# Holding the split of the first group's x in fixed order at the end of its step, in a recurrence with a feed-forward block

## The chip, the cores and the metric

One core of a Trainium2 chip. The metric is the device time of one execution, in microseconds (us).

The engines in the profile: PE is TensorE (its matmuls; PEld are its weight loads), DVE is VectorE, ACT is ScalarE, POOL is GpSimd, and SP is the sync engine, whose queue issues most loads. L405 is line 405 of the kernel before. The granted clock (PEclk) is the share of its full clock that PE was given; "half clock" is a share of 0.5.

## The reference

```python
# q, k, v, alpha: (4, 8, 768, 48) float32; w1, w2: (384, 1024); w3: (1024, 1024); w_out: (1024, 384), float64
state = zeros((B, H, D, D))
for t in range(S):                                   # S = 768
    state = alpha[:, :, t, :, None] * state + einsum('bhd,bhe->bhde', k[:, :, t], v[:, :, t])
    y[:, :, t] = einsum('bhd,bhde->bhe', q[:, :, t], state)
x = y.transpose(0, 2, 1, 3).reshape(3072, 384)
out = (((x @ w1) * (x @ w2)) @ w3) @ w_out           # (3072, 384)
```

## The kernel before

The recurrence runs in 24 steps, one per chunk of 128 rows of one batch. Step n works on several chunks at once: scores of chunk n, transposes of chunk n+1, logarithms and decays of chunks n+3 and n+4. Four chunks make a group g of x, which goes out to DRAM in `attend` and comes back transposed with `load_x`. `split_x` splits it into three parts for exact matmuls: one operation on ACT (L405) and two on DVE (L406, L407). A *gate piece* is nine matmuls (six L416, three L420) on these parts. Gate pieces are pushed between the steps of the recurrence by `run`. The weights come as 64-bit words and are converted in `to_fp32`, a few instructions at a time (`convert`).

The order of instructions in the source is a priority, not the final order. A scheduler places each instruction when its own plan says that its inputs are ready. `keep_order(True, instruction)` holds an instruction at its place in the source. Each engine then works through its own list in order (the prediction shows it on ACT).

```python
def to_fp32(dst, *srcs):
    # ... raw tile, loads on the sync queue
    first = st.setdefault("raw", 0) < 3              # only three conversions are held in order
    st["raw"] += 1
    keep_order(first, nc.scalar.activation(rest, low, AF.Copy, scale=2.0 ** -52))        # L201
    # ... L202, L206 on DVE, L208 on ACT, then L210 to L213 on DVE; ends in L221 (ACT), L223, L224 (DVE)

def attend(n):
    # ...
    for half in range(2):
        if g:
            later.append((to[half, :, :, ds(c * C, C)], x[ds(DP * half, D)]))            # sync queue, next step
        else:
            nc.gpsimd.dma_start(out=to[half, :, :, ds(c * C, C)], in_=x[ds(DP * half, D)])  # POOL's queue

def load_x(g, queue=nc.sync):
    st["xT", g] = xp.tile([C, KM, TG], FP32, tag="xT", name="xT")
    queue.dma_start(out=st["xT", g], in_=xd[g].rearrange("(k p) t -> p k t", p=C))       # L399

def split_x(g, i):
    x = st.pop(("xT", g))
    t = tr[i].tile([C, 3, KM, TG], FP32R, tag="x3", name="x3")
    st["x3", g] = t
    nc.scalar.activation(t[:, 0], x, AF.Copy, scale=1.0 - 2.0 ** -13)                    # L405
    nc.vector.tensor_sub(t[:, 1], x, t[:, 0].bitcast(FP32))                              # L406
    nc.vector.scalar_tensor_tensor(t[:, 2], t[:, 0].bitcast(FP32), 1.0 + 1.0 / P, x,     # L407
                                   op0=ALU.mult, op1=ALU.subtract)

for n in range(N + 1):
    # ... store(), loads of later chunks
    if n:
        attend_state(n - 1)                          # L375
    if n < N:
        scores(n)                                    # L356 on PE, L359 on DVE
    transposed(n + 1)                                # L316 on PE, L318 on ACT
    if n - 2 in begin:                               # group 0: n = 6
        g, tiles = begin[n - 2]
        split_x(g, 0)
        fill.extend(gate(g, f) for f in tiles)
    pieces = ((0, 0, 1), (1, 1, 1), (1, 1, 0), (1, 1, 0))[(n - 6) % 4] if n > 5 else (0, 0, 0)
    # ... logs
    decayed(n + 2)                                   # L294 on DVE, from q and k
    convert(1, 2 if n == 0 else 3)
    advance(n)
    if n in begin:
        load_x(begin[n][0], nc.gpsimd)               # group 0: n = 4
    if n:
        attend(n - 1)                                # L381 on PE, L385 on ACT
    outer(n)                                         # L328 on PE
    run(pieces[0])
    convert(n > 0)
    run(pieces[1])
    decays(n + 3)                                    # L278 on PE, L284 and L285 on ACT
    convert(n < 9)
    run(pieces[2])
```

## Time and profile before

| what | before |
|---|---|
| time, median of 3 runs | 495.98 us (494.5 to 497.73) |
| PE busy in the profiled execution | 469.7 us of 496.0 us |
| the one long wait: ACT at L405 for x of group 0 | 8.1 us, ending at 54.05 us |
| from the scores (L356) of step 5 to those of step 6 | 11.7 us |
| from step 6 to step 7, and from 7 to 8 | 8.2 us and 8.9 us |

Every step has one group of sixteen L356 matmuls, so their starts are a clock for the recurrence. A step that takes 11.7 us where its neighbours take 6 to 9 has a hole. The profile's lines are in the prediction below. A list of waits has, for each engine and line, what released it, then the total wait, how often, and the longest. A timeline has the start in us from the span's start, the duration, engine, line, operation, output and input, and in brackets the idle time just before and what ended it.

### The profile page before, as it was taken

The page shows a single profiled execution, that of the slowest core. Times are in us where ns is not written, and L with a number is a line of the kernel's source. Part 1 is how long each engine was busy: PE and PEld are TensorE (multiplying, and loading weights), DVE is VectorE, ACT ScalarE, POOL GpSimd, SP SyncE. Part 2 cuts the span into 40 slices and gives each one's busy share as a digit, 9 for nine tenths or more (in the row PEclk, how much of TensorE's full clock was granted, in tenths as well). Part 3 has the DMA queues.
Part 4 walks back from the last instruction along what each step waited for, and adds up shares of the span by engine and source line. Part 5 has one row for each costly group of instructions (what it writes and reads, how often), then busy time and mean ns, then how long its engine had stood idle before and what let it go on. Part 6 is the DMA issues. An engine that isn't in the chain of part 4 may idle for free.

```text
span 496.0 us, 9941 instructions
## 1 busy us (share of the span) xinstructions
PE 469.7 (95%) x3774; PEld 427.1 (86%) x3774; DVE 372.1 (75%) x621; ACT 248.2 (50%) x479; POOL 45.8 (9%) x94
## 2 busy tenths in 40 slices
PE   7787599999899989999999999999999999999996
PEld 3566499798899879999999988888888999999996
DVE  3579599999988646999999769686434786677771
ACT  4565577678667443555565445454223533333330
POOL 3244032211302210000000000000000000000000
PEclk9788699999899989999999999999999999999999
DMA  9999999989998823456646433320001885555511
GB/s 169 203 209 223 216 204 260 197 205 222 217 211 183 230 82 112 117 196 197 196 156 196 155 116 113 121 93 32 33 32 51 227 231 176 176 176 175 174 49 48
DMA packets 158255, 79.10 MB, mean 159 GB/s; under 512 B 104640, under 2 KB 151232, under 8 KB 158208
## 3 DMA queue, kind: packets, MB, share of 16 engines
q1 hardware_dynamic: 155920, 74.86, 59.6%
q0 software_dynamic: 2288, 3.62, 2.9%
q8 instruction: 29, 0.48, 0.4%
q14 instruction: 18, 0.15, 0.1%
HBM read 56.40 MB, written 22.06 MB: 158 GB/s over the span
## 4 chain that ended last, share of the span: by engine, by line
PE 69%; DVE 3%; DMA 2%; issue 1%; SPq 1%; ACT 1%; DVEq 0%; ACTq 0%
PE bank L416 36%; PE bank L420 18%; PE bank L465 8%; PE bank L381 2%; DMA raw<-in_moe_w_out_dram 2%; PE bank L459 1%; PE bank L356 1%; PE bank L375 1%; DVE ms L359 1%; PE bank L316 1%; SPq L439 1%; DVE x L407 1%; PE bank L328 0%; DVE x L406 0%; DVE qk L294 0%
## 5 line engine op out<-in xcount | busy, mean ns | idle before, releaser
L416 PE MATMUL bank<-x,w 128*128 128x384 f32 x768 | 160.2, 343 | 1.2 <-DVE ms L359 1.2
L416 PEld LDWEIGHTS bank<-x,w 128*128 128x128 f32 x768 | 134.3, 189 | 6.0 <-DVE ms L359 2.0
L418 ACT ACTIVATE t<-bank 128x384 f32<-128x384 f32 x152 | 74.4, 491 | 113.6 <-PE bank L416 104.3
L421 DVE SCALAR_TENSOR_TENSOR r<-bank,t 128x384 f32<-128x384 f32 x128 | 69.4, 552 | 38.0 <-ACT t L418 27.6
L420 PE MATMUL bank<-x,w 128*128 128x384 f32 x384 | 87.8, 336 | 1.7 <-DVE x L407 1.3
L420 PEld LDWEIGHTS bank<-x,w 128*128 128x128 f32 x384 | 68.2, 188 | 3.1 <-DVE x L407 1.6
L416 PE MATMUL bank<-w3o,ab 128*128 128x384 f32 x384 | 70.4, 334 | 0.0
L416 PEld LDWEIGHTS bank<-w3o,ab 128*128 128x128 f32 x384 | 66.9, 188 | 0.0
L465 PE MATMUL bank<-wo,w3T 128*128 128x384 f32 x128 | 42.6, 486 | 0.0
L201 ACT ACTIVATE rest<-raw 128x512 f32<-128x512 uint32 (+1 forms) x36 | 23.4, 651 | 28.1 <-DMA raw<-in_moe_w_dram 19.7
L356 PE MATMUL bank<-qkT 48*128 48x128 f32 x384 | 31.1, 304 | 6.7 <-ACT qkT L318 6.3
L420 PE MATMUL bank<-w3o,ab 128*128 128x384 f32 x192 | 37.1, 334 | 0.0
L465 PEld LDWEIGHTS bank<-wo,w3T 128*128 128x128 f32 x128 | 24.2, 189 | 14.9
L356 PEld LDWEIGHTS bank<-qkT 48*128 48x128 f32 x384 | 25.8, 203 | 12.6 <-ACT qkT L318 7.2
L484 DVE TENSOR_TENSOR ab<-abl,ab 128x1024 fp32r<-128x1024 f32 x24 | 29.3, 1223 | 9.1 <-ACT ab L483 9.1
L432 DVE TENSOR_TENSOR ab<-r 128x384 f32<-128x384 f32 x64 | 35.4, 553 | 0.9
L483 ACT ACTIVATE ab<-abl 128x1024 fp32r<-128x1024 f32 x24 | 25.5, 1062 | 18.8 <-PE bank L420 18.8
L420 PEld LDWEIGHTS bank<-w3o,ab 128*128 128x128 f32 x192 | 33.6, 188 | 0.0
L208 ACT ACTIVATE power<-power,rebias 128x512 uint32<-128x512 uint32 (+1 forms) x36 | 25.0, 697 | 15.8 <-DVE power L206 15.5
L359 DVE TENSOR_TENSOR ms<-bank,keep 128x512 int32<-128x512 int32 x48 | 30.8, 680 | 1.1 <-PE bank L356 1.1
L294 DVE TENSOR_TENSOR qk<-kq,e 128x768 f32<-128x768 f32 x24 | 22.8, 951 | 11.4 <-ACT e L285 6.4
L318 ACT COPY qkT<-bank 128x512 f32<-128x512 f32 x48 | 25.7, 587 | 10.2 <-PE bank L316 10.2
(74 smaller groups left out, 548.5 us busy)
## 6 DMA issues: line engine op xcount, KB each, us to landing
abd<-ab SPq DMA_DIRECT2D x64, 192.0 KB, 2.5
abl<-abd SPq DMA_DIRECT2D x24, 512.0 KB, 4.5
raw<-in_moe_w_dram SPq DMA_DIRECT2D x16, 512.0 KB, 4.2
raw<-in_moe_w_dram SPq DMA_DIRECT2D x24, 256.0 KB, 4.9
ac<-in_alpha_dram SPq DMA_DIRECT2D x24, 192.0 KB, 4.5
kq<-in_k_dram SPq DMA_DIRECT2D x24, 192.0 KB, 5.0
kq<-in_q_dram SPq DMA_DIRECT2D x24, 192.0 KB, 5.0
v<-in_v_dram SPq DMA_DIRECT2D x24, 192.0 KB, 4.5
```

The lines of the kernel that those rows point to most:

```text
L208: keep_order(first, nc.scalar.activation(power, power, AF.Relu, scale=2.0 ** 23, bias=rebias))
L318: keep_order(n < 2, nc.scalar.copy(qkT[:, :, :, ds(DP * half, DP)], tp[half]))
L356: nc.tensor.matmul(sc[i][:, j, :], qkT[r, 0, j, :], qkT[r, 1, j, :], start=True, stop=True)
L359: nc.vector.tensor_tensor(ms[:, i].bitcast(I32), sc[i].bitcast(I32), keep_bc, op=ALU.bitwise_and)
L416: nc.tensor.matmul(p1, w[part][i], x[part][i], start=(part == i == 0), stop=(part == 1 and i == n - 1))
L418: nc.scalar.activation(t, p1, AF.Copy, scale=(1.0 + 1.0 / P) * scale)
L420: nc.tensor.matmul(p2, w[2][i], x[2][i], start=(i == 0), stop=(i == n - 1))
L421: nc.vector.scalar_tensor_tensor(to, p2, -scale, t, op0=ALU.mult, op1=ALU.add)
L432: nc.vector.tensor_mul(ab, *r)
L465: nc.tensor.matmul(po, w3T[:, j, :], wo[:, j, :], start=(j == 0), stop=(j == KF - 1))
L483: nc.scalar.activation(t[:, 0], ab, AF.Copy, scale=1.0 - 2.0 ** -13)
L484: nc.vector.tensor_sub(t[:, 1], ab, t[:, 0].bitcast(FP32))
```

## The change

The intent is to take the split of group 0 off the place where ACT waits for x. It is moved from the middle of step 6 to its end, and held there so that the scheduler can't place it early. The other splits stay as they were.

```diff
-    def split_x(g, i):
+    def split_x(g, i, fixed=False):
...
-        nc.scalar.activation(t[:, 0], x, AF.Copy, scale=1.0 - 2.0 ** -13)
-        nc.vector.tensor_sub(t[:, 1], x, t[:, 0].bitcast(FP32))
+        keep_order(fixed, nc.scalar.activation(t[:, 0], x, AF.Copy, scale=1.0 - 2.0 ** -13))
+        keep_order(fixed, nc.vector.tensor_sub(t[:, 1], x, t[:, 0].bitcast(FP32)))
...
-    begin = {4 + 4 * g: (g, range(FH if g < 4 else KF)) for g in range(5)}
+    first = 4
+    begin = {first + 4 * g: (g, range(FH if g < 4 else KF)) for g in range(5)}
+
+    def visit(n, fixed=False):
+        g, tiles = begin[n]
+        split_x(g, 0, fixed)
+        fill.extend(gate(g, f) for f in tiles)
...
-        if n - 2 in begin:
-            g, tiles = begin[n - 2]
-            split_x(g, 0)
-            fill.extend(gate(g, f) for f in tiles)
+        if n - 2 in begin and n - 2 > first:
+            visit(n - 2)
...
         convert(n < 9)
+        if n - 2 == first:
+            visit(first, True)
         run(pieces[2])
```

## The prediction

> **What bounds the kernel now.** I read the page first (busy shares, slices, groups), then the list of waits, then the timeline of each engine around the first split of x, and last the busy time by stretch. The kernel has two parts: an attention recurrence of 24 steps (up to about 200 us) with pieces of the feed-forward block pushed between its steps, then the rest of the feed-forward block and the output projection.
>
> The page says that PE is the bound of the whole:
>
> ```profile
> PE 469.7 (95%) x3774; PEld 427.1 (86%) x3774; DVE 372.1 (75%) x621; ACT 248.2 (50%) x479; POOL 45.8 (9%) x94
> PE   7787599999899989999999999999999999999996
> DVE  3579599999988646999999769686434786677771
> PEclk9788699999899989999999999999999999999999
> DMA  9999999989998823456646433320001885555511
> ```
>
> The span less PE's busy time is 26 us of idle PE. One slice is 12.4 us. From slice 5 on PE is nearly full, so what is lost before that isn't made up. The fifth slice (49.6 to 62 us) is the odd one: PE and DVE at half, and a low granted clock. The list of waits for 51 to 58 us says why, as waiting engine, line, releaser, and us in total, times, longest:
>
> ```profile
> ACT x L405 <- DMA xT<-xd: 8.1, 1, 8.1
> DVE w L223 <- ACT w L221: 6.2, 1, 6.2
> PE bank L356 <- ACT qkT L318: 6.0, 1, 6.0
> ```
>
> L405 is the first instruction of the split of x for group 0 (the group's x has gone out to DRAM and is read back transposed). All twelve splits run L405, and this is the only one whose wait shows. The timeline of ACT shows what stood behind it, and the timelines of POOL and PE what it hung on and what hung on it:
>
> ```profile
> 45.41 0.50 ACT L285 ACTIVATE e<-bank 128x384 f32<-128x384 f32 x1
> 54.05 1.16 ACT L405 ACTIVATE x<-xT 128x1152 fp32r<-128x1152 f32 x1 [8.13 <-DMA xT<-xd]
> 55.11 0.61 ACT L221 ACTIVATE w<-mant 128x512 fp32r<-128x512 f32 x1
> 56.18 1.06 ACT L318 COPY qkT<-bank 128x512 f32<-128x512 f32 x2
> ...
> 47.55 0.80 POOL L399 DMA_DIRECT2D xT<-xd  x1 [2.63 <-DMA xd<-x]
> ...
> 57.29 2.08 PE L356 MATMUL bank<-qkT 48*128 48x128 f32 x16 [6.04 <-ACT qkT L318]
> ```
>
> The split belongs to step 6 of the source, but in the emitted order it stands ahead of the L318 copies of step 5 (the transposed q and k of chunk 6, without which the scores of step 6 can't start). So the instruction order is not the source order: whatever places the instructions thought x would be there by 46 us. The load was only issued at 47.55 and landed at 54.0. PE and DVE ran out of work 4 to 5 us after ACT stopped, and all three stood until 54 to 57 us.
>
> Next, what limits the stretches around it (us from:to, length, busy us and count of PE, PEld, DVE, ACT, POOL, then PE clock, DMA share, GB/s):
>
> ```profile
> 38.00:51.30 13.30, 10.29 (x150) 8.15 (x148) 10.75 (x18) 7.04 (x15) 5.56 (x8) 0.87 1.08 233
> 51.30:57.30 6.00, 0.01 (x2) 0.01 (x2) 1.54 (x3) 3.25 (x6) 0.00 (x0) 0.64 0.85 187
> 57.30:64.00 6.70, 6.70 (x68) 6.23 (x69) 6.70 (x11) 4.52 (x12) 1.62 (x3) 0.56 1.05 237
> 64.00:80.00 16.00, 16.00 (x196) 14.83 (x195) 15.84 (x31) 12.45 (x28) 5.16 (x10) 1.00 1.06 208
> 80.00:100.00 20.00, 18.80 (x268) 16.74 (x267) 19.73 (x35) 13.56 (x29) 3.31 (x7) 1.00 1.00 228
> ```
>
> From 57 to 100 us DVE is busy 42.3 of 42.7 us and PE 41.5: both engines have no room. So a microsecond given back to both before that is a microsecond at the end, as far as the loads keep up. DMA is near its limit all along.
>
> **What the Trainium skill says.** (1) "PSUM — Partial Sum Buffer", section "Engine vs sequencer instructions": the queues of ScalarE, VectorE and GpSimd are strict FIFO. The trace agrees: no ACT instruction starts between 45.41 and 54.05, though the L318 copies that follow had had their transposes finished at about 48.0 (PE's L316 ends there). (2) "TensorE: Matmul & The Clock Gate", section "What's actually happening": the array runs at half clock after an idle window of about 3.4 us and at full clock after a busy one. The trace agrees: the clock is 0.56 in 57.3 to 64, and the sixteen L356 matmuls take 2.08 us there against 1.16 at 74 us. (3) "DMA: Bandwidth & Descriptors", section "Specifications": transfers need 512 B or more for full rate. In 44 to 75 us 18,898 of 21,151 packets are under 512 B, and the engines' share is full at a mean of 219 GB/s.
>
> **The change, part by part.** It adds no instruction and takes none away. It moves the split of group 0 alone from the middle of step 6 to its end, and holds its ACT operation (1.16 us) and its first DVE operation (1.35 us) in source order, so they can't be placed early. The other eleven splits stay where they are.
>
> (a) The wait goes. ACT can go on at 45.9 with L221, L201 and the L318 copies; the scores of step 6 can follow at once on PE's L375, which ends at 51.25. DVE gets back up to 6.15 us, PE up to 6.04. Gain up to **6.1 us**. By the end of step 6 (about 58 us on the new timetable: 51.3 plus a step of 6 to 7 us, the spacing of the L356 groups before the wait) the load has been there for 4 us, so the moved split should not wait.
>
> (b) Loads. Before the wait the steps are paced by loads: in the trace's landing records, chunks 6 to 8 of alpha land 0.1, 0.5 and 0.1 us before ACT's L263 reads them. While the engines stood, the sync queue went on issuing (its waits on engines in 44 to 57 us sum to 0.9 us), so after the wait alpha is 5.4, 5.7, 5.3, 5.5 and 4.2 us early for chunks 10 to 14, and the raw weights of the sixth and seventh conversion 3.3 and 4.0 us. That lead was bought by the wait. If all engines move 6 us forward and the transfers don't, the smallest of these fall short by 2 to 3 us. Some comes back, as the sync queue waits on engines for 4 us in 57 to 75 us and for 6 us in 75 to 104, and these waits shorten. ACT and DVE can also go ahead with little queued work. I take **1.6 us** back (a choice between 0 and 3).
>
> (c) The split at the end. The first gate piece needs L405, L406 and, for its last three matmuls, L407: 1.16 + 1.35 + 1.35 = 3.9 us after the last exponential of step 6. Before, these ran in the shadow of the wait and DVE's part pushed the L359 masks to 60.18. If PE takes the gate piece ahead of the scores of step 7 it stands for up to 3 us; if those scores are placed first it loses nothing, and the placement does like to fill holes. I take **0.6 us**.
>
> (d) Clock. With the hole gone the half-clock stretch of 53 to 63 us shortens. PE's step-6 groups took some 2.4 us longer than at full clock, but DVE was full in that stretch, so most was hidden. Gain **0.3 us**.
>
> Sum: 6.1 - 1.6 - 0.6 + 0.3 = 4.2 us, so 495.98 - 4.2 = **491.8 us**.
>
> **Rivals.** R1, the loads take over: alpha, q/k and the raw weights become the pace again in steps 6 to 10. For it: DMA at its limit and the leads of near zero before the wait. Against it: no engine but POOL waits on a DMA from 57 to 160 us, and the leads of 5 us. Gain then 1 to 3 us, 493 to 495. R2, the end of the step becomes the new wait: PE stands for the split chain and DVE for L405. For it: the order is fixed and PE takes its matmuls in order. Against it: independent scores and transposes of step 7 can be put into the hole. Gain then 2 to 3.5 us. R3, everything carries through, clock too: 6 us and up to 2 more, 488 to 490. For it: PE and DVE are full afterwards and the rest of the kernel is PE work of fixed amount. R4, the placement of all later instructions shifts, as it works forward from this point, with a microsecond or two either way; the profile can't tell.
>
> **Range and chances.** The three runs of before lie between 494.5 and 497.7, so the reference itself moves by 1.5 us. R1 and R2 together give the upper end, R3 the lower: **488.5 to 495.5**. Faster by over 2% needs 486.1, that is 9.9 us, more than the whole wait with its clock effect: 0.04. Slower by over 2% needs 10 us of new waits: 0.02. Within 2%: 0.94.
>
> **What would show it.** In the changed profile: the ACT wait on xT at L405 is under 1 us and the split starts at 56 to 60 us; PE's L356 of step 6 starts at 51 to 52 us instead of 57.3; the fifth slice of PE and DVE rises to 8 or 9. For (b): alpha's L263 and the L201 conversions of steps 6 to 9 show DMA waits of 0 to 3 us in all. For (c): a PE wait ahead of the first L416 or L420, on ACT's L405 or on DVE's L406 or L407. For the carrying through: the last attention step ends some 4 us earlier and the part after 200 us keeps its length. I'm wrong if those waits on loads or on the split take over 4 us, if x lands later than now because its load or its stores move in POOL's queue, or if other instructions are placed worse.

## The result

| | before | with the change |
|---|---|---|
| median, 4 runs each | 496.23 us (494.5 to 497.73) | 501.55 us (500.27 to 501.8) |
| ratio of the fast runs | | 1.0103, 95% interval 1.0066 to 1.0141 |
| profiled execution (that of before is a further one) | 497.82 us | 500.27 us |

A ratio here is the mean time of one kernel's fast runs over that of the other's of the same rounds, so it isn't quite the ratio of the medians quoted. The change is slower by 1.0%, inside "within 2%", but on the other side of zero from the prediction of 491.8 us and outside its range. A repeat with more rounds (label after_again) gave 502.48 us against 495.99, ratio 1.0132 (1.0085 to 1.018), as expected; its profile was the 912 us execution and isn't used. The text on record for it:

> The change once more, as a reference for the other three of this batch on the same chip. Both theories: 1.005 to 1.015 of the kernel before, as in the first comparison.

The page of the changed kernel has the same work (busy times of the engines, and rows of tenths by slice):

```profile
PE 470.5 (94%) x3774; PEld 425.2 (85%) x3774; DVE 371.6 (75%) x621; ACT 247.6 (50%) x479; POOL 45.3 (9%) x94
PE   8888389899899999999999999999999999999996
DVE  3578789996967866899999869776434687777771
PEclk9788869999999999999999999999999999999999
```

The hole is still in the fifth slice, and deeper: PE's digit there is a 3, where it was a 5 before and where the prediction asked for 8 or 9. DVE's went from 5 to 7. PE's busy time as a whole is as before (470.5 and 469.7 us), so what the change costs is mostly idle PE (28.0 us against 26.3 in the two traces). A slice of 12.5 us hides what happened inside it, and the windows cut it finer. These are the same stretches as in the prediction (from:to, length, busy us and count of PE, PEld, DVE, ACT, POOL, then PE clock, DMA share, GB/s), of the changed kernel:

```profile
51.30:57.30 6.00, 3.97 (x66) 3.23 (x66) 3.10 (x6) 3.73 (x9) 1.13 (x2) 1.00 0.90 220
57.30:64.00 6.70, 0.80 (x2) 0.80 (x3) 6.67 (x13) 5.50 (x11) 2.44 (x6) 0.58 1.20 222
64.00:80.00 16.00, 15.32 (x147) 13.31 (x148) 13.97 (x24) 8.59 (x18) 2.21 (x4) 0.75 0.93 213
```

PE gained 4.0 us of work in the first stretch and lost 5.9 in the second (0.80 against 6.70 before). The changed kernel's waits for 51 to 70 us say why:

```profile
PE bank L416 <- ACT x L405: 7.5, 1, 7.5
ACT rest L201 <- DMA raw<-in_moe_w_dram: 4.9, 2, 3.1
DVE qk L294 <- ACT qkT L318: 2.9, 1, 2.9
```

ACT's wait on x is gone from this list, and PE has one of 7.5 us on the split instead. PE's timeline shows where it stands. First the kernel before:

```profile
62.88 1.08 PE L278 MATMUL bank<-la,utri 128*128 128x384 f32 x2
63.50 1.52 PE L416 MATMUL bank<-x,w 128*128 128x384 f32 x6
64.86 0.68 PE L420 MATMUL bank<-x,w 128*128 128x384 f32 x3
65.48 1.16 PE L356 MATMUL bank<-qkT 48*128 48x128 f32 x16
```

and the changed kernel:

```profile
51.78 1.16 PE L356 MATMUL bank<-qkT 48*128 48x128 f32 x16 [1.39 <-ACT qkT L318]
...
54.84 0.91 PE L278 MATMUL bank<-la,utri 128*128 128x384 f32 x2
63.20 1.33 PE L416 MATMUL bank<-x,w 128*128 128x384 f32 x3 [7.45 <-ACT x L405]
65.18 1.33 PE L416 MATMUL bank<-x,w 128*128 128x384 f32 x3 [0.65 <-DVE x L406]
66.53 1.30 PE L420 MATMUL bank<-x,w 128*128 128x384 f32 x3
67.76 2.08 PE L356 MATMUL bank<-qkT 48*128 48x128 f32 x16
```

The order on PE is the same in both: decays (L278), first gate piece (L416, L420), then the scores of step 7 (L356). In the kernel before, the split had been done in time and the gate piece ran at once. In the changed one PE reaches the gate piece at 55.75 us and stands there till 63.2, with the scores of step 7 behind it.

ACT's timeline of the changed kernel shows why the split is so late:

```profile
53.91 1.11 ACT L318 COPY qkT<-bank 128x512 f32<-128x512 f32 x2
58.17 0.68 ACT L201 ACTIVATE rest<-raw 128x512 f32<-128x512 uint32 x1 [3.14 <-DMA raw<-in_moe_w_dram]
58.75 0.62 ACT L221 ACTIVATE w<-mant 128x512 fp32r<-128x512 f32 x1
...
61.56 0.52 ACT L267 CAST la<-la 128x384 fp32r<-128x384 f32 x1
61.96 1.18 ACT L405 ACTIVATE x<-xT 128x1152 fp32r<-128x1152 f32 x1
```

L405 carries no wait: x was there. But ahead of it in ACT's order stands L201, the first ACT operation of the sixth weight conversion. The source has it in step 7, the scheduler had placed it ahead of the held split, and its raw weights landed only at 58.09 (it starts at 58.17). ACT stood 3.14 us for them and then worked 3.8 us (58.17 to 61.96) on other things before the split came.

DVE's two operations of the split end at 60.3 us in the kernel before (57.64 and 58.91, 1.35 us each), and at 66.4 in the changed one:

```profile
55.08 0.96 DVE L294 TENSOR_TENSOR qk<-kq,e 128x768 f32<-128x768 f32 x1 [2.90 <-ACT qkT L318]
...
63.77 1.35 DVE L406 TENSOR_TENSOR x<-xT,x 128x1152 fp32r<-128x1152 f32 x1
65.04 1.35 DVE L407 SCALAR_TENSOR_TENSOR x<-x,xT 128x1152 fp32r<-128x1152 f32 x1
```

The wait ahead of L294 is put down to ACT's L318, which ended at 55.02. But a semaphore instruction of DVE just before L294 waits for q and k of chunk 8, and in the trace's landing records q of chunk 8 lands at 54.95; DVE gets past this instruction at 55.03. So up to 54.95 the wait is one on a load, and only the last 0.1 us can be ACT's.

The starts of the scores, in us after the first matmul (1.2 us less than in the timelines), give the whole account:

| scores of step | 5 | 6 | 7 | 8 | 9 | 14 | 20 | 23 | last instruction |
|---|---|---|---|---|---|---|---|---|---|
| before | 44.4 | 56.1 | 64.3 | 73.2 | 80.7 | 118.9 | 165.3 | 190.2 | 494.8 |
| change | 43.5 | 50.6 | 66.6 | 77.4 | 84.8 | 123.3 | 172.3 | 192.7 | 497.2 |
| difference | -0.8 | -5.5 | +2.3 | +4.2 | +4.1 | +4.3 | +7.0 | +2.4 | +2.4 |

By step 6 the change is 5.5 us ahead: 4.7 us are won from step 5 to 6 (7.0 us instead of 11.7), and 0.8 us it was ahead at step 5 already, before anything differs. Then 7.8 us are lost from step 6 to 7 (16.0 us instead of 8.2), and another 1.9 from 7 to 8 (10.8 instead of 8.9). From there the difference is carried on, moving between 2.4 and 7.0 us. The two profiled executions differ by less (2.4 us) than the medians (5.3), since the profiled execution of before was a slow one among its runs and that of the change its fastest.

### The profile page after: what moved, and what is told of

Read it like the earlier page. It is cut to its first block, busy times and chain, and to the rows that moved or that the text cites.

```text
span 498.5 us, 9954 instructions
## 1 busy us (share of the span) xinstructions
PE 470.5 (94%) x3774; PEld 425.2 (85%) x3774; DVE 371.6 (75%) x621; ACT 247.6 (50%) x479; POOL 45.3 (9%) x94
## 4 chain that ended last, share of the span: by engine, by line
PE 74%; DVE 9%; DMA 8%; issue 4%; ACT 3%; SPq 1%; POOL 1%; ACTq 0%; DVEq 0%; POOLq 0%
PE bank L416 37%; PE bank L420 18%; PE bank L465 8%; DMA raw<-in_moe_w_out_dram 3%; PE bank L356 2%; DMA raw<-in_moe_w_dram 2%; PE bank L381 2%; DVE qk L294 2%; DVE ms L359 2%; PE bank L459 1%; PE bank L316 1%; DMA kq<-in_k_dram 1%; PE bank L146 1%; PE bank L375 1%; DMA dec<-ends 1%
## 5 line engine op out<-in xcount | busy, mean ns | idle before, releaser
L416 PE MATMUL bank<-x,w 128*128 128x384 f32 x768 | 160.5, 343 | 11.2 <-ACT x L405 7.5
L416 PEld LDWEIGHTS bank<-x,w 128*128 128x128 f32 x768 | 134.5, 189 | 16.7 <-ACT x L405 8.1
L420 PE MATMUL bank<-x,w 128*128 128x384 f32 x384 | 88.3, 337 | 2.3 <-DVE x L407 1.3
L420 PEld LDWEIGHTS bank<-x,w 128*128 128x128 f32 x384 | 68.4, 189 | 4.3 <-PE bank L416 2.4
L416 PE MATMUL bank<-w3o,ab 128*128 128x384 f32 x384 | 70.4, 334 | 0.0
L416 PEld LDWEIGHTS bank<-w3o,ab 128*128 128x128 f32 x384 | 66.9, 188 | 0.0
L201 ACT ACTIVATE rest<-raw 128x512 f32<-128x512 uint32 (+1 forms) x36 | 23.4, 651 | 34.0 <-DMA raw<-in_moe_w_dram 25.7
L420 PE MATMUL bank<-w3o,ab 128*128 128x384 f32 x192 | 37.1, 334 | 0.0
L356 PE MATMUL bank<-qkT 48*128 48x128 f32 x384 | 32.3, 309 | 2.2 <-ACT qkT L318 1.7
L356 PEld LDWEIGHTS bank<-qkT 48*128 48x128 f32 x384 | 26.9, 208 | 8.5 <-issue 4.0
L420 PEld LDWEIGHTS bank<-w3o,ab 128*128 128x128 f32 x192 | 33.6, 188 | 0.0
L294 DVE TENSOR_TENSOR qk<-kq,e 128x768 f32<-128x768 f32 x24 | 22.9, 953 | 14.3 <-ACT e L285 8.3
L318 ACT COPY qkT<-bank 128x512 f32<-128x512 f32 x48 | 25.7, 591 | 9.2 <-PE bank L316 9.0
```

Of the source, the lines that this page charges most:

```text
L294: nc.vector.tensor_mul(qks[n % 3][:, :, :, 0:D], st.pop(("kq", n)), st.pop(("e", n)).rearrange("p i (h d) -> p i h d", h=H))
L318: keep_order(n < 2, nc.scalar.copy(qkT[:, :, :, ds(DP * half, DP)], tp[half]))
L356: nc.tensor.matmul(sc[i][:, j, :], qkT[r, 0, j, :], qkT[r, 1, j, :], start=True, stop=True)
L416: nc.tensor.matmul(p1, w[part][i], x[part][i], start=(part == i == 0), stop=(part == 1 and i == n - 1))
L420: nc.tensor.matmul(p2, w[2][i], x[2][i], start=(i == 0), stop=(i == n - 1))
```

## The experiments

**Theories.** *Order*: holding the split makes everything in ACT's queue ahead of it part of its path, and PE takes the gate piece ahead of the scores; the loss is this chain. *Loads* (rival): work moved forward, transfers didn't, so the wait comes back at loads of q, k and raw weights. *Clock* (rival): PE's idle time sits just ahead of a dense stretch, and the half clock after it is what costs. *Placement* (rival): something elsewhere was placed worse. The texts number theories: T1 is order, T2 loads alone, T3 PE's order alone, T4 clock, and T5 that the end of the split sets the time. Rounds are three for the first six and five for the rest, and "before" is the kernel before in the same rounds on the same chip. Edits are against the change where not said otherwise. Step starts are from one traced execution each. In the traces of kernels whose order is the same up to step 5, the scores of that step start at 42.9 to 45.2 us, so a difference of one or two microseconds between two traces isn't safe.

### 1. Which half of the change acts: place or hold

**end_free**: the split at the end of the step, but not held.

```diff
-            visit(first, True)
+            visit(first, False)
```

> The split moved to the end of the step but not held in order. In the built order its ACT operation stands where it stood before the change, so both theories expect the wait of about 8 us on the load of x and the time of the kernel before, 495 to 498 us: the hold in order, not the place in the source, is what acts.

Measured: 496.58 us (496.09 to 497.73), ratio 0.9994 (0.9936 to 1.0051). Compared with the kernel before, the order is the same on all engines but DVE, where the split's two operations and their neighbours have changed places (L407 ends at 63.65 us instead of 60.26). The old waits are there (46 to 80 us):

```profile
ACT x L405 <- DMA xT<-xd: 7.6, 1, 7.6
...
PE bank L356 <- ACT qkT L318: 7.2, 1, 7.2
```

So the move in the source does nothing to the time by itself. The result comes from the hold.

**mid_fixed**: the split held at its old place in the middle of step 6.

```diff
-        if n - 2 in begin and n - 2 > first:
-            visit(n - 2)
+        if n - 2 in begin:
+            visit(n - 2, n - 2 == first)
...
-        if n - 2 == first:
-            visit(first, True)
```

> The change with the split left at its old place in the middle of step 6, but held in order there. In the built order the split's ACT operation then stands right behind the copies of the transposed q and k of chunk 7 and ahead of the conversion that waits for raw weights. Theory T1 (the change loses because the split stands in ACT's queue behind a conversion that waits for its load and behind the rest of step 6, while PE takes its first gate matmuls in order ahead of the scores of step 7): the split starts at 54 to 57 us, PE's wait ahead of the first L416 falls from 7.5 us to 1 to 4 us, the scores of step 7 start at 60 to 65 us after the first matmul instead of 66.6, total 490 to 496 us, below the change by 6 us or more. Rival T2 (the loads alone set the pace of steps 6 to 8 and no order can beat it): the scores of step 7 start at 66 us or later and the total stays at 499 to 502.

Measured: 497.85 us (497.46 to 498.96), ratio 1.0013 (0.9946 to 1.0081). The split starts at 54.1 us after the first matmul (change: 60.8), and the gate piece stands for less:

```profile
PE bank L416 <- DVE x L406: 2.6, 1, 2.6
```

Scores of step 7 at 62.2 and of step 8 at 72.4, earlier than before by 2.1 and 0.8 us. The steps behaved as expected, the total (490 to 496) didn't: it is level with before. Against the change this is 3.7 us better by the medians, which are of different rounds (by the ratios, 1.0013 and 1.0103, about 0.9%). So a longer queue ahead of the held split is part of the loss.

### 2. The consumer: is the gate piece ahead of the scores the loss?

**gate_late**: the change, with the first gate piece moved from the end of step 6 into step 7.

```diff
-        pieces = (...)[(n - 6) % 4] if n > 5 else (0, 0, 0)
+        pieces = (...)[(n - 6) % 4] if n > 7 else (2, 1, 1) if n == 7 else (0, 0, 0)
```

> The change, with the first gate piece run in step 7 (two pieces there after its outer products) and not at the end of step 6, so that PE takes the scores, transposes and attention of step 7 before it. T1: PE's 7.5 us wait ahead of the first L416 shrinks to 2 to 5 us, the scores of step 7 start at 55 to 58 us after the first matmul, and the total is 494 to 498 us, 3 to 7 us under the change. T2 (loads alone): the time lost moves to waits of ACT and DVE on loads in step 7, and the total stays within 2 us of the change's 501.5.

Measured: 497.02 us (496.5 to 497.93), ratio 1.0001 (0.9944 to 1.0058). The scores of step 7 start at 57.4 instead of 66.6, and the wait ahead of the gate piece shrinks:

```profile
DVE qk L294 <- DMA kq<-in_q_dram: 3.5, 1, 3.5
...
PE bank L416 <- ACT x L405: 1.6, 1, 1.6
```

The ranges that the theory of order gave for the total and for step 7 hold, and the wait is shorter than the 2 to 5 us expected. But the scores of step 8 start at 74.2, 1.0 us later than before: the split is no earlier (63.27 us, in the change 61.96), and all of the gate work of the two steps now stands ahead of the scores of step 8.

**before_gate_late**: the control, the same edit on the kernel before.

> Control: the kernel before, with the first gate piece after the outer products of step 7 and nothing else. There the split is done by the time PE gets to the gate piece, so moving it should neither win nor lose: 495 to 499 us, ratio 0.995 to 1.006. If it wins 1% by itself, the gain seen with the gate piece moved is not the undoing of the change's loss but a gain of its own.

Measured: 495.0 us (494.09 to 499.94), ratio 0.9993 (0.9944 to 1.0041). The edit by itself is worth nothing, so what it gives back on top of the change is a loss of the change.

**mid_gate_late** and **mid_gate_late5** (a repeat with five rounds): the edits of mid_fixed and gate_late together.

> Both edits: the split held in order in the middle of step 6, and the first gate piece after the outer products of step 7. T1: no PE wait over 2 us at 55 to 65 us, the 5.5 us won at the scores of step 6 are kept to the end apart from load waits, total 488 to 493 us. T2: 496 us or more.

> The version with the split held in the middle of step 6 and the first gate piece in step 7, once more with five rounds: its four runs lay between 493 and 500 us, though its traced run was 4.6 us ahead of the traced run of before. Theory T5 (what counts is when the split is done and with it the gate pieces, not when ACT's wait on x is gone: in the traces the split's last operation ends 59.1 us after the first matmul before, 65.2 in the change, 64.9 with both places undone at the end of the step, 61.1 here): 0.988 to 0.997 of before. Otherwise 0.997 to 1.006.

Measured: 498.15 us (493.21 to 500.04), ratio 1.0007 (0.9926 to 1.0087), and 496.48 (493.96 to 499.77), ratio 0.9992 (0.995 to 1.0034). Both traces show scores of step 8 some 4.5 us earlier than before (68.3 and 68.8), but the traced executions took 493.21 and 494.82 us, the fastest of four and the third of six, and others of the same kernel took up to 500. An expectation of 488 to 493 was missed, and the repeat (by T5 0.988 to 0.997) doesn't support a gain. A warning: a trace of one execution told a better story than the mean of the runs.

### 3. The queue ahead: the conversion that was placed before the split

**hold_conv**: the change, with the sixth conversion held in source order too, so it can't stand ahead of the split.

```diff
-        first = st.setdefault("raw", 0) < 3
+        first = st.setdefault("raw", 0) < 3 or st["raw"] == 5
```

> The change, with one weight conversion (the sixth, which the source begins in step 7) held in source order too. In the built order it then no longer stands ahead of the split on ACT, and its DVE operations no longer ahead of L406; PE's order is that of the change. Theory T1 (the conversion's wait for raw weights, pulled up ahead of the held split, delays it): the ACT wait of 3.1 us ahead of the split goes, PE's wait ahead of the first L416 falls from 7.5 us to 3 to 5 us, the scores of step 7 start 3 to 4 us earlier than in the change (62 to 64 us after the first matmul), total 3 to 5 us under the change of this batch. Theory T3 (PE's order alone): the wait stays over 6 us and the total within 1.5 us of the change.

Measured: 499.3 us (497.47 to 499.78), ratio 1.0051 (1.0006 to 1.0096), in the same rounds as after_again's 502.48: 3.2 us better. But the waits between 50 and 70 us are not what was expected:

```profile
PE bank L416 <- ACT x L405: 7.0, 1, 7.0
ACT w L221 <- DVE mant L213: 4.2, 1, 4.2
...
DVE qk L294 <- DMA kq<-in_q_dram: 3.1, 1, 3.1
```

The wait on raw weights is gone. In its place DVE waits 3.1 us for q and k of chunk 8 (here the list names the load), and ACT waits 4.2 us for DVE ahead of the split. The PE wait was expected to be 3 to 5 us and stays at 7.0, and the scores of step 7 start at 64.8, not at 62 to 64: one queue was cleared, and the next thing in it was late as well. The total is in the range expected, but how the 3.2 us come about isn't shown: the scores of steps 6, 7 and 8 start 1.2, 1.8 and 1.9 us earlier than in the change.

**hold_gate_late**: both, the sixth conversion held and the gate piece late.

> The same with the first gate piece after the outer products of step 7. If the held order costs through both the conversion ahead of the split and the gate piece ahead of the scores, both undone give most of the predicted gain: 490 to 494 us, under the kernel before by 2 to 6 us, with no PE wait over 2 us between 50 and 70 us. If loads take what the order gives: within 2 us of the kernel before.

Measured: 495.49 us (492.98 to 496.79), ratio 0.9978 (0.9934 to 1.0022). The expected 490 to 494 was missed; the value lies in the range given for loads (within 2 us of before), which x_later_both below tests. The scores of step 7 start at 57.8 but those of step 8 at 74.2, as in gate_late. The two edits take back the whole loss, and no more.

**mid_gl_hold**: the edits of mid_gate_late and hold_conv.

> The same with the sixth conversion held as well, so that on DVE its two operations no longer stand ahead of the split's and wait for raw weights there. T5: the split's last DVE operation ends at 57 to 60.5 us after the first matmul, the scores of step 8 start at 66 to 69 us, total 0.982 to 0.994 of before. If the end of the split doesn't set it: 0.996 to 1.004 as for the other versions.

Measured: 494.9 us (492.42 to 496.21), ratio 0.9951 (0.9917 to 0.9986). Split in the middle, held; gate piece late; conversion held: half a per cent under before, just above the range of T5 (0.982 to 0.994) and just below that of its rival. The split's last operation ends in its range (60.4 us after the first matmul); the scores of step 8 start at 70.4, 2.8 us earlier than before, but not at 66 to 69.

### 4. Rival: the loads

**before_wide** and **after_wide**: in both kernels the loads of q, k, v and alpha take rows of 1536 bytes, of the same total size but of the wrong data (wrong result), so transfers should be quicker.

```diff
-        b, c = divmod(n, NCH)
-        return src[b, :, ds(c * C, C), :].rearrange("h p d -> p h d")
+        flat = src.rearrange("b h s d -> (b h s) d").rearrange("(m h) d -> m h d", h=H)
+        return flat[ds(n * C, C)]
```

> Wrong result on purpose: the kernel before, with the loads of q, k, v and alpha reading rows of 1536 contiguous bytes in place of 192-byte ones (same bytes, fewer and larger packets), so that loads no longer set the pace of the attention steps. The instruction order shifts a little with it. Both theories: total 3 to 15 us under the kernel before; a wait of ACT on the load of x of 3 to 10 us stays, as that load hangs on the stores of x and on the order in POOL's queue, not on traffic.

> Wrong result on purpose: the change with the same wide loads. If waits on loads are what turned the gain into a loss (ACT's conversion waiting for raw weights, DVE for q and k), the gain comes back: 3 to 6 us under the wide kernel before. If PE's order (gate piece ahead of the scores of step 7, behind a split at the end of ACT's step) costs it regardless of loads, it ends within 2 us of the wide kernel before or above it, with a PE wait of 3 us or more ahead of the first L416.

Measured: before_wide 502.16 us (501.64 to 503.6), ratio 1.0132 (1.0099 to 1.0165), slower than before, against expectation; ACT there waits 9.8 us on x. after_wide 495.25 us (494.1 to 496.68), ratio 0.9989 (0.9955 to 1.0024), with 5.2 us of PE wait ahead of L416. The pair (6.9 us apart) would speak for loads, but the instruction orders came out different as well: in the traces on ACT in 19 places and on DVE in 46 between before and before_wide, and in 30 and 40 between the change and after_wide. So I count this pair as inconclusive: an edit that changes the scheduler's plan is not a clean test of transfers.

**x_later** and **x_later_both**: the 576 KB load of x of group 0 issued later, behind the loads of q and k of chunk 8 that it shares the DMA engines with: on the change at 54.2 us instead of 47.0 (x_later), on hold_gate_late at 53.1 instead of 46.8 (x_later_both). Up to some 185 us nothing else changes place.

```diff
+        if n == 8:                                   # in decays, ahead of load_ends
+            load_x(0, nc.gpsimd)
...
-        queue.dma_start(out=st["xT", g], in_=xd[g].rearrange("(k p) t -> p k t", p=C))
+        keep_order(g == 0, queue.dma_start(out=st["xT", g], in_=xd[g].rearrange("(k p) t -> p k t", p=C)))
...
-        if n in begin:
+        if n in begin and n > first:
```

> The change, with only the load of x of group 0 issued later: behind the store of the exponentials of chunk 8 in POOL's queue, so at about 53.5 us in place of 47, when the held split starts at 62 us anyway. Up to 200 us no other instruction of any engine changes place. Load theory (the 576 KB of x collide with q and k of chunk 8 and with the raw weights, which DVE and ACT then wait for, 2.9 and 3.1 us): DVE's wait ahead of the q/k product of chunk 8 falls under 1 us, ACT's wait on raw weights ahead of the split under 1.5 us, the split starts 1 to 3 us earlier or waits for x itself until about 60 us, the scores of step 7 start at 63 to 66 us after the first matmul, total 1 to 4 us under the change. If the collision does not matter: both waits stay near 3 us and the total within 1 us.

> The same later load of x in the version with the sixth conversion held and the first gate piece in step 7 (0.998 of before, where DVE still waited 3.6 us for q and k of chunk 8). Load theory: that wait falls under 1 us, the scores of step 7 start 2 to 4 us earlier than 57.8, and the total is 490 to 494 us, 0.988 to 0.996 of before: the gain predicted for the change. If loads are not what took it: 0.996 to 1.002.

Measured: x_later 501.75 us (500.26 to 506.32), ratio 1.0098 (1.006 to 1.0136); x_later_both 496.31 (494.79 to 498.95), ratio 0.9989 (0.9951 to 1.0027). The wait on q and k falls from 2.9 to 1.3 us in the first and from 3.6 to 1.2 in the second (two lines are added, so L294 is L296 here):

```profile
DVE qk L296 <- DMA kq<-in_q_dram: 1.2, 1, 1.2
```

So the x load does delay q of chunk 8: its load takes 6.0 us from issue to landing in x_later and 8.2 in the change, 6.8 in x_later_both and 8.5 in hold_gate_late. The wait on raw weights ahead of the split falls too, from 3.1 to 1.6 us in x_later. But the totals don't move: in x_later the scores of step 7 start at 66.6 as in the change, and in x_later_both they start 3.2 us earlier than in hold_gate_late, those of step 8 only 2.1 us (1.1 us ahead of before). The collision is real and isn't what sets the time.

### 5. Rival: the clock

**warm**: the change, with 28 filler matmuls on zeros just ahead of the held split, so PE doesn't idle.

```diff
         if n - 2 == first:
+            busy(28)
             visit(first, True)
```

> The change, with 28 matmuls on zeros (results unused) put on PE between the last decay matmuls of step 6 and the first gate piece, some 6 us of PE work inside its 7.5 us wait, so that the clock stays granted. The order is otherwise that of the change but for a few later swaps. Theory T4 (a part of the loss is the half clock that the wait brings on in step 7): the clock stays at 1.0 over 58 to 72 us, the scores of step 7 start where they do in the change (66 to 67 us after the first matmul), those of step 8 2 to 3.5 us earlier (74 to 75.5 instead of 77.4), total 2 to 4 us under the change, 498 to 500 us. If the clock is hidden behind DVE and loads as in the kernel before: total within 1 us of the change.

Measured: 501.96 us (501.16 to 504.26), ratio 1.0127 (1.0089 to 1.0166). The filler (L146) lies in the hole, and the scores of step 7 take 1.16 us, where they took 2.08 in the change:

```profile
58.55 6.20 PE L146 MATMUL bank<-zeros 128*128 128x512 bf16 x27 [0.42 <-DVE ms L359]
...
68.65 1.16 PE L356 MATMUL bank<-qkT 48*128 48x128 f32 x16
```

By the trace's clock records the change has a stretch of 13.7 us at half clock that begins at 58.4 us (before: 10.2, beginning at 53.0); here the one such stretch from 45 us on is 3.4 us, beginning at 53.2. The step from 7 to 8 takes 8.9 us, as before, instead of 10.8. And the total is that of the change. In this trace the split comes 1.4 us later (63.36), so only 1.0 of the 1.9 us is left at step 8. The clock costs its 1.9 us there and then, but taking it away doesn't bring the end forward.

### 6. A version that beats both

**early_x**: the kernel before, with the x stores of group 0 on the sync queue like those of the other groups. The idea was to have x earlier.

```diff
-            if g:
+            if True:
```

> The kernel before, with the stores of x of group 0 on the sync queue like those of the other groups, so that they don't stand in POOL's queue behind its waits on the decay loads (the last pair of stores was issued 6 us after x had been written). In the built order the split then stands behind the copies of chunk 6 without being held. If the late load of x is the root of the wait, the ACT wait at the split falls from 8.1 us to under 3, and the total is 489 to 495 us. If the loads pace these steps anyway: 495 to 499.

Measured: 494.41 us (493.32 to 495.33), ratio 0.9973 (0.9944 to 1.0003). The total lies in the range expected (489 to 495), but the idea was wrong: POOL issues the load of x at 52.48 us, later than before (47.55); ACT waits 3.0 us for it. What it does is to change the scheduler's order. The split now stands behind the L318 copies of the next chunk without any hold, so the scores of step 6 start at 48.0, but PE waits 5.8 us on L405 ahead of the gate piece.

**early_x_mid**: that, with the edits of mid_gate_late (against the kernel before).

> The same stores on the sync queue, with the split held in order in the middle of step 6 and the first gate piece after the outer products of step 7. Root theory: 487 to 493 us. Loads alone: 495 to 499.

Measured: **491.24 us** (489.23 to 493.3), ratio 0.9906 (0.9874 to 0.9939), the fastest of all kernels here. Its waits for 50 to 70 us:

```profile
ACT x L405 <- DMA xT<-xd: 3.8, 1, 3.8
...
PE bank L416 <- ACT qkT L318: 1.5, 1, 1.5
```

x is later still (issued at 53.77, split at 60.42 in the timeline), ACT waits for it, and it hardly matters: the scores of step 7 start at 54.5, and PE has all of step 7 to do before it comes to the gate piece. No DVE wait on q and k is left in this stretch. The order built is the same as that of early_x with the gate piece late and no hold at all (built for comparison, not run), so the hold has no part in this gain: it is the stores' queue together with the gate piece's place.

**early_x_mid_hold**: with all first twelve conversions held as well (`< 12` in place of `< 3`).

> The best so far (stores of x of group 0 on the sync queue, split held in the middle of step 6, first gate piece in step 7, 0.9906 of before) with all twelve weight conversions held in source order. T1: conversions no longer stand ahead of the attention steps with a wait for their load, another 0 to 4 us: 487 to 492 us. Against it: held conversions leave holes on ACT and DVE, 492 to 496 us.

Measured: 492.25 us (490.92 to 496.03), ratio 0.993 (0.9881 to 0.9979). No further gain, as the text's second range (492 to 496) has it.

## Why the prediction was wrong

**(a) The wait goes: right.** ACT no longer waits for x, and the scores of step 6 start 5.5 us earlier, 4.7 of it won in the step itself, where 6.1 was predicted. The split found x there, as predicted, though it started at 61.96 us and not at 56 to 60.

**(b) Loads take 1.6 us back: right in kind, larger, and on other loads than named first.** The waits that return are 3.1 us on raw weights ahead of the split (4.9 in two waits; the prediction had these on its list) and 2.9 us on q of chunk 8. R1 names q and k, but the prediction read its leads from alpha and the raw weights alone. Together they pass the 4 us that it gave as a sign of being wrong. The load of q had been slow before the change too (issue to landing 8.7 us, with 8.2 in the change), but nobody was there to wait for it.

**(c) The end of the step takes 0.6 us: this is the step that failed.** The prediction wrote "If PE takes the gate piece ahead of the scores of step 7 it stands for up to 3 us", then chose 0.6 in the hope that the scores would be placed first. PE does take the gate piece first, as it did before, and stands 7.45 us ahead of it and 0.65 in it. Two things were mis-sized. The order: the kernel before already had the gate piece ahead of the scores, which its timeline showed, and nothing in the change gave the scheduler a reason to turn it. The length: the chain was counted from the last exponential (3.9 us of split), and not from where ACT's queue stood. Ahead of the held L405 were 3.14 us of waiting for raw weights and 3.8 us of other work, the last exponential of step 6 (L285, which ends at 61.68) among it; from there to the end of the split it is 4.7 us, near the 3.9 counted. PE had done its own work of step 6 by 55.75. The rival R2 named the mechanism and gave it at most 4.1 us of loss (2 us of gain left of 6.1); the step lost 7.8.

**(d) Clock, a gain of 0.3: wrong sign, without effect on the end.** The half-clock stretch grew from 10.2 to 13.7 us. (Over the whole trace it didn't: before has two later stretches of 3.4 us that the change lacks, and the mean granted clock is 0.969 and 0.973.) "TensorE: Matmul & The Clock Gate", section "Terms", of the Trainium skill puts the penalty at about the throttled time times (1 - K/N); at half rate that gives an estimate of 6.9 us for 13.7. But in 4.8 us of these, up to 63.2, PE stood idle. Run warm took most of this throttled time away and left the total where it was.

**"A microsecond given back to both before that is a microsecond at the end": not borne out.** It needed both engines to move forward together. The scores moved, but the split's last DVE operation went from ending at 60.3 to 66.4 us, and the gate work that fills PE afterwards hangs on that. The end of the split alone doesn't set the total either: it is at 67.5 in gate_late, level with before, and at 64.3 in early_x_mid, the fastest.

**What is shown and what stays open.** Shown: the hold acts and not the place (end_free); the loss is given back by moving the consumer (gate_late, level with before), and about 3 us of it, by the medians, by clearing the queue (hold_conv); both together are level with before too; the same consumer edit on the kernel before gives nothing. Also shown: taking away the collision of loads, or the half clock, each alone, doesn't move the total. Not tested by a run of its own: placement. In the traces the order of the change differs from that of before in 19 places on ACT and 36 on DVE, from the split on, and gate_late and hold_conv move later instructions too, so they aren't perfectly clean either. Against it: the whole difference is there at step 8 (4.2 us) and is still 4.3 at step 14, and up to step 8 PE's order is that of before. Open: why the versions with both places mended end level with before and don't keep the 5.5 us. In gate_late and hold_gate_late the scores of step 7 are over 6 us early and those of step 8 are 1.0 us late; the first gate matmul starts at 64.5 and 63.0 us there and at 63.5 before, so no gate work was won. In mid_gate_late, where step 8 is early too in the traces, the mean of the runs still isn't better. Runs of the kernel before spread from 493.4 to 499.9 us over all rounds, so a microsecond or two of such an effect can't be told from the spread with these rounds. Nor is it shown why early_x_mid, 2.7 us ahead at step 8, is 6.4 us ahead at step 23 and 6.8 at the end of its trace (5.0 by the medians).

## What to carry to other kernels

Holding an instruction in an in-order queue makes everything that is queued before it, with the loads that it waits for, part of its path: count that queue from the timeline, not the instruction's own chain, and look whether its consumer stands ahead of independent work on the other engine. If the producer is moved later, move the consumer with it. And test a shift with several rounds and a control on the old kernel: one trace of a fast execution looked like a gain that the runs didn't have.

## What the Trainium skill lacked or had wrong

- "Perfetto Trace Analysis", section "Optimization Strategy", says to find the gap on the engine that matters, find what blocks it, and have that start sooner or end faster. It lacks that in queues served in order a wait that is removed can come back at the next consumer: 8.1 us of ACT on x became 7.45 us of PE on the split, and the time rose by 1.0%.
- "TensorE: Matmul & The Clock Gate", section "Terms": its penalty (throttled time times 1 - K/N) gives an estimate of 6.9 us for the 13.7 us at half clock. The runs gave 1.9 us in the step concerned and nothing in the total (501.96 us with the clock kept up, 501.55 and 502.48 without). It lacks that throttled time in which PE stands idle (4.8 of the 13.7 us here) costs nothing, and that the rest counts only where PE sets the pace.
- "DMA: Bandwidth & Descriptors", section "Anatomy of one DMA — SWDGE (gpsimd) path", fits a transfer with 2.0 us and its bytes over 436 GB/s. For the 576 KB load of x, which goes that way, this gives an estimate of 3.4 us; the trace of the change has 7.4 from issue to landing, and 5.7 as the median of five such loads, with the DMA engines' share at 1.11 and 0.90 in the two stretches of the first of these. The fit has no term for other loads in flight.
